# Scores from small square tiles, a rotated query layout, and a reordered start of the expert stage

## The chip, the cores and the metric

The kernel runs on one core of one Trainium2 chip. The metric is device time in microseconds (us). The core has TensorE (PE in the profile, with PEld for its weight loads), VectorE (DVE), ScalarE (ACT), GpSimd (POOL) and SyncE (SP), which issues most transfers. Each engine works through its own instructions in order, and waits where an operand or a buffer is not ready.

## The reference, cut to what matters

Three stages are computed one after the other: attention through a memory of 32 slots per head, a dense layer pair with ELU, and a layer with eight experts of which each token uses one.

```python
# attention: 8 batches x 8 heads, 576 rows, head size 64, 32 memory slots
a = softmax(phi, axis=rows)
k_m, v_m = a.T @ k, a.T @ v                  # 32 x 64 per head
attn = softmax(q @ k_m.T / 8)                # 576 x 32 per head
x = attn @ v_m                               # heads side by side: 4608 x 512
# dense: w_in 512 x 2048, w_out 2048 x 512 (given in double precision)
x = elu(x @ w_in) @ w_out
# experts: e = argmax of x @ w_gate, for each token
out = softmax(x @ w_gate)[e] * (relu(x @ w1[e]) @ w2[e])
```

## The kernel before, in words

**First part, attention and dense layer.** The work goes through 8 batches `b`; each has two halves `g` of 288 rows, and each half 16 steps `f` over slices of 128 of the 2048 inner columns. One step is `mm1` (L488, 6 matmuls of 288 columns, L496), `elu` and `split_g` on ACT, DVE and POOL, and `mm2` (L518, 12 matmuls, L528). `mm1` runs two steps ahead of `mm2`. A value is split in a rounded part and a rest, so that three fast products give a full-precision one. Beside the steps of batch b run, in small pieces, the attention of batch b+1 (`attn_items`, L725: pairs of a step and a function, for steps 0 to 31) and the rows of the finished half (`y_items`, L745: logits, ranks, and three `y_row` that turn 96 rows each and write them to a table in memory).

**Attention pieces.** Heads come in two groups u of four. `load_q` (L206) brings the queries of a group, 32 partitions per head, into half of a buffer `big`, of which there are two; `a4t` (L387) turns them in blocks of 32x32 on DVE into the other half (L390). `a3` (L355) sums keys and values per memory slot, `a3b` (L368) scales them into `kvm` on DVE (L372) and turns the keys block by block (L378) onto the diagonal of a 128x128 tile `bdk`, which is zero elsewhere. `a4` (L393) makes the scores: for each of two row halves g, two matmuls of the whole 128x128 array and 288 columns (L402), then a DVE transpose out of PSUM (L405). `a3c` (L380) turns the values on PE (L383) once both groups are scaled. `a6n` (L482) later multiplies the turned values by slices of w_in (`m_tiles`, L450, L458). In full precision each of these matmuls shows as two records in the trace.

**Order.** For batch 0, and the start of batch 1, the order is the written list `START`; `LATER` gives a few more pieces for steps of the rest of batch 1's work. From step 24 of the sequence on the kernel only lists the pieces; a scheduler of the framework orders each engine's instructions by what it believes to be ready, and earlier listed ones first. The order in the trace there is its own, not that of the list. Around the end of the last batch the order is written out again.

**PSUM.** The pool `ps_m` has two banks, shared by every piece beside `mm1` and `mm2`: the sums of `a3`, the scores, the turned values, the products of `a6n` (two banks at once), the logits, and `y_row`, whose bank ACT empties (L643).

**Second part, experts.** Tokens have been put in lists per expert (`itab`, written by `y_scatter`). Two blocks of 128 tokens ("early" slots) of the first expert are done before the full lists are known: their first products `early_mm1`, the turning of the result `early_hpose`, their second products `early_mm2`. The full lists are fetched by an indirect transfer into `its` (L1003), turned on PE by `columns` (L1053, L1057) into the index columns, and then `gather` (L1064) fetches the tokens of the next slots. `ctl_a`, `ctl_b`, `ctl_c` compute on DVE the control table that the engines read into registers for each slot. In the loop over slots, `slot(j)` runs `mm1` (L1098) and `mm2` of 128 tokens.

The calls at this seam, L1157 to L1175, and later L1209:

```python
split_lo(1, [0, 1, 3], first)      # POOL for even chunks, DVE for odd ones
split_lo(1, [2], first, V)
early_hpose(0)
...                                # early_mm1(1, 1, c)
columns()
gather(0)
split_lo(1, [4, 5, 7, 6], first)
gather(1); gather(2)
ctl_a(); ctl_b()
early_mm2(0); early_hpose(1); xpose(0); ctl_c()
early_mm2(1)                       # after the helpers of slot are defined
```

Of the kernel before, what the change touches and what calls it, by code (L numbers as in the profile page):

```python
# [24 lines left out]

START = """
q.0 phi.0 x.0 a1.0 kv.0 a1e.0 A0.0 a2.0.0 phi.1 A1.0.0 A1.0.1 a1.1 x.1 q.1 R.0.1 a4t.0 R.0.0 B.0 a2.0.1 a3.0 a1e.1
a2.1.0 kv.1 a3b.0 A0.1 a4t.1 A1.1.0 A1.1.1 R.1.0 x.2 a2.1.1 a4.0.0 a4.0.1 a5.0 a5e.0 a3.1 a3b.1 a5b.0 A0.2 R.1.1
a5m.0 a5c.0 a4.1.0 a5d.0 a4.1.1 x.3 a5.1 A1.2.0 A1.2.1 R.2.1 C.1 a5e.1 R.2.0 a3c A0.3 D.1.1 x.4 a5b.1 a5m.1 A1.3.0
A1.3.1 R.3.0 B.2 a5c.1 R.3.1 D.1.0 A0.4 A1.4.0 a5d.1 x.5 M.0 A1.4.1 x.6 R.4.1 R.4.0 C.3 B.4 D.3.0 Me.0 A0.5 A1.5.0  # L30
A1.5.1 R.5.1 D.3.1 mm1.0 R.5.0 mm1.1 A0.6 A1.6.0 A1.6.1 R.6.0 R.6.1 C.5 D.5.1 M.1 elu.0 elu.1 Me.1 g.0 M.2 Me.2
mm1.2 x.7 x.8 A0.7 x.9 A1.7.0 B.6 R.7.0 D.5.0 A1.7.1 g.1 elu.2 mm1.3 mm2.0 mm2.1 M.3 elu.3 Me.3 R.7.1 x.10 mm1.4
# [10 lines left out]
n.a5e.0 n.a3.1 n.a3b.1 n.a3c  # L43
"""
LATER = {
    23: "n.a5b.0 n.a5m.0 n.q2",
    24: "n.M.0 n.a5c.0",
    25: "n.pk2 n.a4.1 n.a5.1 n.a5e.1 n.a5b.1",
    27: "n.M.1",
    29: "n.a5d.0",  # L50
    30: "n.a5m.1 n.a5c.1 n.a5d.1",
# [6 lines left out]
def attn_moe_moe2_kernel(  # L58
# [13 lines left out]
    nc = tc.nc  # L72
# [89 lines left out]
    with ExitStack() as order:  # L162
        order.enter_context(tc.manual_schedule())
        setup()
        with ExitStack() as p1, ExitStack() as late_pool:
# [11 lines left out]
            wo = [  # L177
                wt0.rearrange("p y c a n -> p (y c) a n")[:, :, 1], pool.tile([P, NF, DM], F32R, name="wol"),
            ]
            bdk = pkp.tile([P, 2, P], F32, name="bdk")  # L180
            kvm = pkp.tile([P, 2, NQ, D], F32, name="kvm")

            win_t = {}
# [21 lines left out]

            def load_q(b, u):  # L206
                t = big()
                nc.sync.dma_start(out=t[:, 0], in_=q[b, 4 * u:4 * u + 4].rearrange("h (s j) d -> (h s) (j d)", j=NJ))
                q_t[b, u] = t

            conv_x, conv_h = {}, {}
# [156 lines left out]
            def a3b(b, u):  # L368
                ps, rs = st.pop(("kv", b, u)), st.pop(("rs", b, u))
                nc.vector.tensor_scalar(out=rs, in0=rs, scalar1=1e-9, scalar2=None, op0=ALU.add)  # L370
                nc.vector.reciprocal(out=rs, in_=rs)
                nc.vector.tensor_scalar(  # L372
                    out=kvm[:, :, u], in0=ps[:, 0:P].rearrange("p (y d) -> p y d", y=2), scalar1=rs, scalar2=None,
                    op0=ALU.mult,
                )
                for h in range(4):
                    r = slice(32 * h, 32 * h + 32)
                    nc.vector.transpose(out=bdk[r, :, r], in_=kvm[r, 0, u])  # L378

            def a3c(b):  # L380

# [8 lines left out]
                nc.vector.transpose(out=qT, in_=qt[:, 0].rearrange("p (j b d) -> p j b d", j=NJ, b=2))  # L390
                st["qT", b, u] = qT

            def a4(b, u, gs=range(2)):  # L393
                qT = st["qT", b, u]
                if gs[0] == 0:
                    st["sT", b, u] = pool.tile([P, NJ, M], F32, tag="aT", name="sT")
                sT = st["sT", b, u]
                n = NJ // 2
                for g in gs:
                    ps = ps_m.tile([P, 512], F32, tag="m", name="ps_s")  # L400
                    for db in range(2):
                        nc.tensor.matmul(  # L402
                            ps[:, 0:G], bdk[:, db, :], qT[:, n * g:n * g + n, db, :], start=(db == 0), stop=(db == 1)
                        )
                    nc.vector.transpose(out=sT[:, n * g:n * g + n], in_=ps[:, 0:G])  # L405

            def a5(b, u):
                sT = st["sT", b, u]
# [225 lines left out]

            def y_row(b, g, i):

                last = (b, g) == (B - 1, 1) and i > 0
                yr = (pool if last else late["p"]).tile([PK, DM], F32, tag=("yr", "a", "aT")[i * last], name="yr", bufs=1 if last else YR)
# [86 lines left out]
            def attn_items(b):  # L725

                t = [2, 3, 5, 5, 5, 4, 6, 7, 9, 9, 8, 10, 12, 11]
                t += [22, 23, 24, 26, 13, 22]
                it = [
                    (t[0], lambda: (a1(b, 0), a1e(b, 0))), (t[1], lambda: a2(b, 0)), (t[2], lambda: a3(b, 0)),  # L730
                    (t[2], lambda: load_pk(b, 1)), (t[3], lambda: a3b(b, 0)),
                    (t[4], lambda: (a1(b, 1), a1e(b, 1))), (t[5], lambda: a4t(b, 0)), (t[5], lambda: load_q(b, 1)),
                    (t[6], lambda: a2(b, 1)), (t[7], lambda: a4(b, 0)),
                    (t[8], lambda: a3(b, 1)), (t[9], lambda: (a3b(b, 1), a3c(b))),
                    (t[10], lambda: (a5(b, 0), a5e(b, 0))), (t[11], lambda: (a5b(b, 0), a5m(b, 0))),
                    (t[12], lambda: (a5c(b, 0), a5d(b, 0))), (t[13], lambda: a4t(b, 1)), (t[14], lambda: a4(b, 1)),
                    (t[15], lambda: (a5(b, 1), a5e(b, 1))), (t[16], lambda: (a5b(b, 1), a5m(b, 1))),
                    (t[17], lambda: (a5c(b, 1), a5d(b, 1))),
                ]
                if b + 1 < B:  # L740
                    it += [(t[18], lambda: load_pk(b + 1, 0)), (t[19], lambda: load_q(b + 1, 0))]
                it += [(NF + 4 * kk + 2, lambda kk=kk: a6n(b, kk)) for kk in range(NSL // 2)]
                return it

# [30 lines left out]
            def at(i, fn):  # L775
                bg.setdefault(i, []).append(fn)

            nc.gpsimd.memset(bdk, 0.0)
            todo = {}
            for u in range(2):  # L780
                for name, fn in (
                    ("phi", load_phi), ("kv", load_kv), ("q", load_q), ("a1", a1), ("a1e", a1e), ("a3", a3), ("a3b", a3b),
                    ("a4t", a4t), ("a5", a5), ("a5e", a5e), ("a5b", a5b), ("a5m", a5m), ("a5c", a5c),
                    ("a5d", a5d),
                ):
                    todo[f"{name}.{u}"] = lambda fn=fn, u=u: fn(0, u)
                for g in range(2):
                    todo[f"a2.{u}.{g}"] = lambda u=u, g=g: a2(0, u, [g])
                    todo[f"a4.{u}.{g}"] = lambda u=u, g=g: a4(0, u, [g])
# [29 lines left out]
            todo["n.q2"] = lambda: load_q(2, 0)  # L819
# [101 lines left out]
def phase2(nc, tc, a):  # L921
# [52 lines left out]
    with ExitStack() as p2:  # L974
# [148 lines left out]

        turn = [0]

        def mm2(get, half, at, ot=None):
            ps = ps_tile(ps_acc, f"acc{2 + turn[0]}")
            turn[0] = 1 - turn[0]
            i = 0
            for f in range(NF2):  # L1130
                for h, y in ((0, 0), (1, 0), (0, 1)):
                    nc.tensor.matmul(ps, get(h, f), half(wt[1][y][f]), start=(i == 0), stop=(i == 3 * NF2 - 1))  # L1132
                    i += 1
            if ot is None:
# [13 lines left out]

            hpose(src, lambda y, g: early_chunk(y, 2 * s + g))

        def early_mm2(s):
            def get(y, f):
                return early_chunk(y, 2 * s + f // 4)[:, P * (f % 4):P * (f % 4) + P]

            mm2(get, first, early_w[:, s:s + 1], early_f32(4 + s))

        split_hi(1, range(NCH), first)  # L1157
        for c in range(NC):
            early_mm1(1, 0, c)
        split_lo(1, [0, 1, 3], first)  # L1160
        split_lo(1, [2], first, V)
        early_hpose(0)
        for c in range(NC):
            early_mm1(1, 1, c)
        columns()
        gather(0)
        split_lo(1, [4, 5, 7, 6], first)
        gather(1)
        gather(2)
        ctl_a()  # L1170
        ctl_b()
        early_mm2(0)
        early_hpose(1)
        xpose(0)
        ctl_c()  # L1175
        def load_regs(j, cols, engines):
            return [
                nc.values_load(ctl[j:j + 1, c:c + 1], engines=engines, min_val=0, max_val=m) for c, m in cols  # L1178
# [27 lines left out]
            for i, (w, c) in enumerate(((w1, cv0), (w2, cv1))):  # L1206
                load_raw(nc, raw[i], w, ev, c)

        early_mm2(1)  # L1209
        cv, = load_regs(0, ((5, 1),), [SP])  # L1210
        ev = nc.values_load(ctl1[0:1, 0:1], engines=[SP], min_val=0, max_val=E - 1)
        for i, w in enumerate((w1, w2)):
# [62 lines left out]
```

## Time and profile before

| | before |
|---|---|
| median of 3 runs | 1434.15 us (1429.45 to 1438.15) |
| the profiled execution | 1433.82 us, of which 1431.8 us from the first to the last instruction |
| mean granted clock of TensorE | 0.969 of full speed |
| PE busy | 1311.6 us, 92% |
| DVE, ACT, POOL busy | 629.5, 636.0, 445.1 us |

The table gives busy time summed over all stages. The first 175 us are the start (written order, batch 0, conversion of the weights); from there to about 926 us run the steps; 926 to 953 us is the seam; from 953 us on the expert slots run.

### The profile page before, as it was taken

What the parts mean: (1) busy time and instruction counts of PE and PEld (TensorE: products, weight loads), DVE (VectorE), ACT (ScalarE), POOL (GpSimd) and SP (SyncE); (2) the same over time, 40 slices, a digit from 0 to 9 for tenths busy, and PEclk for the clock granted to TensorE, in tenths of its full rate; (3) what the DMA queues carried; (4) which work ended last, traced back from release to release, by engine and by line L of the source; (5) the groups of instructions that cost most, each with busy time, mean ns of one, the idle gap of its engine ahead of it and who ended that gap; (6) DMA issues with size and microseconds to landing.
All of it is one profiled execution on the core that took longest, in us unless ns stands there. A gap on an engine that the chain in (4) does not pass through costs nothing. (4 is left out here: it accounts for less than half of the span.)

```text
span 1431.8 us, 26774 instructions
## 1 busy us (share of the span) xinstructions
PE 1311.6 (92%) x9023; PEld 1139.3 (80%) x9023; DVE 629.5 (44%) x1337; ACT 636.0 (44%) x1377; POOL 445.1 (31%) x483
## 2 busy tenths in 40 slices
PE   3478799999999999899999989889999999999996
PEld 2267688898888898799899889768888888888885
DVE  4988564443443443434433323445222555252221
ACT  3567355564565555455555546414111444141110
POOL 2645343343343433333334334231111111111111
PEclk9699999999999999999999999989999999999998
DMA  9646655325324333323431500135111334211110
GB/s 243 186 153 185 204 100 139 87 82 100 87 82 100 100 79 91 109 77 106 108 73 38 164 20 25 23 133 200 39 38 46 121 142 152 101 40 38 44 46 30
DMA packets 55062, 140.68 MB, mean 98 GB/s; under 512 B 8809, under 2 KB 21226, under 8 KB 51312
## 3 DMA queue, kind: packets, MB, share of 16 engines
q1 hardware_dynamic: 46768, 118.15, 29.3%
q0 software_dynamic: 8128, 20.50, 4.4%
q8 instruction: 82, 1.34, 0.4%
q14 instruction: 84, 0.69, 0.2%
HBM read 253.79 MB, written 24.02 MB: 194 GB/s over the span
## 5 line engine op out<-in xcount | busy, mean ns | idle before, releaser
L513 POOL TENSOR_TENSOR gl<-e,gh 128x288 fp32r<-128x288 f32 x242 | 196.1, 813 | 395.8 <-ACT gh L512 316.2
L528 PE MATMUL ps_acc<-gl,wt 128*128 128x288 f32 x1024 | 308.1, 301 | 10.2 <-DVE gl L513 5.0
L528 PE MATMUL ps_acc<-gh,wt 128*128 128x288 f32 x1024 | 306.9, 300 | 3.3 <-ACT gh L512 3.3
L528 PE MATMUL ps_acc<-gh,wol 128*128 128x288 f32 x1024 | 305.6, 298 | 0.0
L496 PE MATMUL ps_h<-ath,wt 128*128 128x288 f32 x1024 | 262.7, 313 | 18.3 <-DVE e L505 18.3
L505 DVE SCALAR_TENSOR_TENSOR e<-e,ps_h 128x288 f32<-128x288 f32 x256 | 114.6, 449 | 257.2 <-ACT e L504 225.4
L496 PEld LDWEIGHTS ps_h<-ath,wt 128*128 128x128 f32 x1024 | 182.1, 193 | 56.2 <-issue 26.9
L528 PEld LDWEIGHTS ps_acc<-gl,wt 128*128 128x128 f32 x1024 | 196.6, 192 | 14.7 <-DVE gl L513 8.3
L528 PEld LDWEIGHTS ps_acc<-gh,wt 128*128 128x128 f32 x1024 | 197.1, 192 | 4.5 <-ACT gh L512 3.8
L528 PEld LDWEIGHTS ps_acc<-gh,wol 128*128 128x128 f32 x1024 | 196.7, 192 | 0.5 <-issue 0.5
L1098 PE MATMUL ps_h<-wt,xh 128*128 x592 | 195.0, 400 | 0.7 <-ACT hh L1114 0.7
L512 ACT CAST gh<-e 128x288 fp32r<-128x288 f32 x256 | 110.0, 431 | 154.7 <-DVE e L505 152.3
L1137 POOL DMA_INDIRECT out_dram<-ot,idw x37 | 37.8, 1021 | 384.0 <-DVE ot L1136 358.1
L496 PE MATMUL ps_h<-atl,wt 128*128 128x288 f32 x512 | 153.9, 301 | 0.0
L503 ACT ACTIVATE e<-ps_h 128x288 f32<-128x288 f32 x256 | 105.1, 410 | 92.4 <-PE ps_h L496 81.4
L1098 PEld LDWEIGHTS ps_h<-wt,xh 128*128 128x128 f32 x592 | 111.2, 188 | 26.1 <-ACT hh L1114 0.6
L1132 PE MATMUL ps_acc<-wt1h,hh 128*128 x296 | 120.9, 409 | 5.7 <-PEq L1178 5.7
L1132 PE MATMUL ps_acc<-wt1h,hl 128*128 x296 | 119.2, 403 | 0.0
L1114 ACT CAST hh<-ps_acc 128x512 fp32r<-128x512 f32 x74 | 39.8, 590 | 174.7 <-PE ps_acc L1112 174.6
L1132 PE MATMUL ps_acc<-wt1l,hh 128*128 x296 | 117.0, 395 | 0.0
L1098 PE MATMUL ps_h<-wt,xl 128*128 x296 | 116.9, 395 | 0.0
L504 ACT ACTIVATE e<-e 128x288 f32<-128x288 f32 x256 | 113.8, 444 | 7.0
(243 smaller groups left out, 1860.5 us busy)
## 6 DMA issues: line engine op xcount, KB each, us to landing
raw<-in_moe_w_dram SPq DMA_DIRECT2D x78, 2048.0 KB
win<-win_s SPq DMA_DIRECT2D x28, 1024.0 KB
big<-in_q_dram SPq DMA_DIRECT2D x16, 576.0 KB
kv<-in_k_dram SPq DMA_DIRECT2D x16, 576.0 KB
kv<-in_v_dram SPq DMA_DIRECT2D x16, 576.0 KB
table<-yr SPq DMA_DIRECT2D x144, 64.0 KB
big<-in_moe_w_out_dram SPq DMA_DIRECT2D x10, 512.0 KB
phi_t<-in_phi_dram SPq DMA_DIRECT2D x16, 288.0 KB
```

The lines of the kernel that those rows point to most:

```text
L496: nc.tensor.matmul(ps, x[:, u, fo:fo + P], y[:, u], start=(n == 0), stop=(n == 3 * NQ - 1))
L503: nc.scalar.activation(out=e, in_=ps, func=AF.Relu, scale=-1.0)
L504: nc.scalar.activation(out=e, in_=e, func=AF.Exp, scale=-1.0)
L505: nc.vector.scalar_tensor_tensor(out=e, in0=e, scalar=-1.0, in1=ps, op0=ALU.add, op1=ALU.max)
L512: nc.scalar.copy(out=gh, in_=e)
L513: eng.tensor_tensor(out=gl, in0=e, in1=gh.bitcast(F32), op=ALU.subtract)
L528: nc.tensor.matmul(acc[c], x[:, f, P * c:P * c + P], y, start=(first and n == 0), stop=(final and n == 2),)
L1098: nc.tensor.matmul(ps, x[:, c], half(wt[0][y][2 * c + hf]), start=(i == 0), stop=(i == 3 * NC - 1))
L1114: nc.scalar.copy(out=h, in_=ps)
L1132: nc.tensor.matmul(ps, get(h, f), half(wt[1][y][f]), start=(i == 0), stop=(i == 3 * NF2 - 1))
L1137: nc.gpsimd.indirect_dma_start(out=out, out_offset=IndirectOffsetOnAxis(ap=at, axis=0), in_=ot, in_offset=None, bounds_check=NT - 1, oob_i ...
```

## The change: what it does

Queries: `load_q` now brings the second row half of each group with its heads rotated by one place (head h in partitions 32((h+1) mod 4) on), in three transfers in place of one. In the list the load of the next batch's group 0 stands at step 8, one after the scores of the same group, and that of group 1 at step 23, one after the scores of group 1; before they stood at steps 22 and 4 (of the next batch).

Scores: `bdk` and its zeroing go. `a3b` writes `kT`: all four heads' keys in one transpose, and a second copy, rotated as the queries are, in four. `a4` uses 32x32 tiles: for each of two inner halves db, each g and each head a matmul of 288 columns, 16 in all, with g=0 in one PSUM bank and g=1 in the other; the two transposes out come after all of them.

Values: `a3c` is listed at step 10, no longer at 9 beside `a3b`.

Seam: all `split_lo` of the second weights go to DVE; `early_mm2(0)`, with `early_hpose(1)` inside it after its f=4, and `early_mm2(1)` are issued ahead of `xpose(0)`; `columns`, the gathers and `ctl_c` are issued inside `early_mm2(1)` after its f=3. The last two `y_row` use the same buffers as the others.

```diff
 def load_q(b, u):
     t = big()
-    nc.sync.dma_start(out=t[:, 0], in_=q[b, 4 * u:4 * u + 4].rearrange("h (s j) d -> (h s) (j d)", j=NJ))
+    src = q[b, 4 * u:4 * u + 4].rearrange("h (s j) d -> h s (j d)", j=NJ)
+    n = NJ * D // 2
+    for g, x, h, k in ((0, 0, 0, 4), (1, 1, 0, 3), (1, 0, 3, 1)):
+        nc.sync.dma_start(
+            out=t[32 * x:32 * (x + k), 0, n * g:n * g + n],
+            in_=src[h:h + k, :, n * g:n * g + n].rearrange("h s f -> (h s) f"),
+        )
 def a3b(b, u):
...
+    nc.vector.transpose(out=kT[:, 0], in_=kvm[:, 0, u])
     for h in range(4):
-        r = slice(32 * h, 32 * h + 32)
-        nc.vector.transpose(out=bdk[r, :, r], in_=kvm[r, 0, u])
+        x = 32 * ((h + 1) % 4)
+        nc.vector.transpose(out=kT[x:x + 32, 1], in_=kvm[32 * h:32 * h + 32, 0, u])
 def a4(b, u):
...
-    for g in gs:
-        ps = ps_m.tile([P, 512], F32, tag="m", name="ps_s")
-        for db in range(2):
-            nc.tensor.matmul(
-                ps[:, 0:G], bdk[:, db, :], qT[:, n * g:n * g + n, db, :], start=(db == 0), stop=(db == 1)
-            )
-        nc.vector.transpose(out=sT[:, n * g:n * g + n], in_=ps[:, 0:G])
+    ps = [ps_m.tile([P, 512], F32, tag="m", name="ps_s") for _ in range(2)]
+    for db in range(2):
+        for g in range(2):
+            for h in range(4):
+                r, m = slice(32 * ((h + g) % 4), 32 * ((h + g) % 4) + 32), slice(32 * h, 32 * h + 32)
+                nc.tensor.matmul(
+                    ps[g][m, 0:G], kT[r, g, db], qT[r, n * g:n * g + n, db, :],
+                    start=(db == 0), stop=(db == 1),
+                )
+    for g in range(2):
+        nc.vector.transpose(out=sT[:, n * g:n * g + n], in_=ps[g][:, 0:G])
 def attn_items(b):
...
-    (t[4], ...), (t[5], lambda: a4t(b, 0)), (t[5], lambda: load_q(b, 1)),
+    (t[4], ...), (t[5], lambda: a4t(b, 0)),
-    (t[8], lambda: a3(b, 1)), (t[9], lambda: (a3b(b, 1), a3c(b))),
+    (t[8], lambda: a3(b, 1)), (t[9], lambda: a3b(b, 1)), (t[9] + 1, lambda: a3c(b)),
-    it += [(t[18], lambda: load_pk(b + 1, 0)), (t[19], lambda: load_q(b + 1, 0))]
+    it += [..., (t[7] + 1, lambda: load_q(b + 1, 0)), (t[14] + 1, lambda: load_q(b + 1, 1))]
 # the seam
-split_lo(1, [0, 1, 3], first)
-split_lo(1, [2], first, V)
+split_lo(1, range(3), first, V)
 early_hpose(0)
+split_lo(1, range(3, NCH), first, V)
 for c in range(NC):
     early_mm1(1, 1, c)
-columns()
-gather(0)
-split_lo(1, [4, 5, 7, 6], first)
-gather(1)
-gather(2)
 ctl_a()
+early_mm2(0, {4: [lambda: early_hpose(1)]})
 ctl_b()
-early_mm2(0)
-early_hpose(1)
+early_mm2(1, {3: [columns, lambda: gather(0), lambda: gather(1), lambda: gather(2), ctl_c]})
 xpose(0)
-ctl_c()
...
-early_mm2(1)
```

## Rows read from the trace of the kernel before

**Rows 1.** The page: span, and busy time by engine.
```profile
span 1431.8 us, 26774 instructions
PE 1311.6 (92%) x9023; PEld 1139.3 (80%) x9023; DVE 629.5 (44%) x1337; ACT 636.0 (44%) x1377; POOL 445.1 (31%) x483
```
**Rows 2.** Busy time by stretch: stretch, length, PE, PEld, DVE, ACT, POOL, granted clock, DMA.
```profile
175.00:926.00 751.00, 719.43 (x5898) 656.27 (x5897) 313.84 (x819) 416.14 (x970) 285.74 (x339) 0.99 0.33 87
926.00:936.00 10.00, 0.45 (x2) 0.02 (x1) 0.91 (x2) 0.00 (x0) 2.73 (x2) 0.75 0.06 9
953.00:1416.00 463.00, 457.05 (x2194) 373.58 (x2192) 170.66 (x265) 124.93 (x228) 75.07 (x74) 1.00 0.25 88
```
**Rows 3.** Waits of PE, whole span: waiter, releaser, us in total, times, longest.
```profile
PE ps_v L383 <- DVE kvm L372: 6.4, 6, 1.3
...
PE ps_v L383 <- ACT yr L643: 0.7, 1, 0.7
...
PE ps_m L1057 <- DVE its L1055: 9.7, 1, 9.7
```
**Rows 4.** Timeline around 446 us: start, length, engine, line, operands, [idle before, releaser].
```profile
445.75 1.34 DVE L390 STREAM_TRANSPOSE big<-big 128x1152 f32<-128x1152 f32 x1
447.01 0.31 DVE L372 TENSOR_SCALAR kvm<-ps_kv,rs 128x128 f32<-128x128 f32 x1
447.47 0.30 PE L383 MATMUL ps_v<-ident,kvm 128*128 128x128 f32 x1 [1.19 <-DVE kvm L372]
```
**Rows 5.** Timeline around 482 us: scores of group 1, then the products of `a6n`.
```profile
481.41 2.11 PE L402 MATMUL ps_s<-big,bdk 128*128 128x288 f32 x8
483.45 1.73 PE L458 MATMUL ps_M<-win,vT 64*32 64x512 f32 x16
483.56 0.48 DVE L405 STREAM_TRANSPOSE sT<-ps_s 128x288 f32<-128x288 f32 x1 [0.49 <-PE ps_s L402]
```
**Rows 6.** Timeline of PE around 408 us: `a6n` with both banks free.
```profile
407.62 1.09 PE L458 MATMUL ps_M<-win,vT 64*32 64x512 f32 x16
408.64 0.40 PE L496 MATMUL ps_h<-ath,wt 128*128 128x288 f32 x1
```
**Rows 7.** Timeline around 538 us: scores of group 0 behind a `y_row`.
```profile
537.95 2.17 PE L402 MATMUL ps_s<-big,bdk 128*128 128x288 f32 x8
538.15 0.68 ACT L643 ACTIVATE yr<-ps_y,r_gate 96x512 f32<-96x512 f32 x1
```
**Rows 8.** Timeline around 486 us: a query load and its transpose.
```profile
483.55 0.35 SPq L208 DMA_DIRECT2D big<-in_q_dram  x1
489.94 1.38 DVE L390 STREAM_TRANSPOSE big<-big 128x1152 f32<-128x1152 f32 x1 [2.77 <-DMA big<-in_q_dram]
```
**Rows 9.** Waits of DVE, 200 to 860 us.
```profile
DVE big L390 <- DMA big<-in_q_dram: 17.6, 5, 5.3
```
**Rows 10.** Waits of PE, 280 to 700 us.
```profile
PE ps_h L496 <- DVE e L505: 12.3, 7, 3.9
```
**Rows 11.** Timeline of the seam, 922 to 952 us.
```profile
922.38 1.88 DVE L997 TENSOR_TENSOR wt1l<-raw,wt1h 128x512 fp32r<-128x512 f32 x3
923.44 3.01 PE L715 MATMUL ps_h<-wt 128*128 128x512 f32 x12
931.63 1.46 POOL L1003 DMA_INDIRECT its<-itab,rowi  x1 [9.40 <-issue]
935.75 0.22 DVE L1055 CAST its<-its 43x128 f32<-43x128 int32 x1 [8.57 <-DMA its<-itab,rowi]
936.93 1.38 POOL L1064 DMA_INDIRECT xg<-table,idx  x1 [2.54 <-DVE idw L1059]
942.67 0.16 DVE L963 SCALAR_TENSOR_TENSOR tmp<-en,ind 128x8 f32<-128x8 f32 x1
950.93 0.15 DVE L1051 CAST ctl<-e 128x1 int32<-128x1 f32 x1
952.32 0.39 PE L1098 MATMUL ps_h<-wt,xh 128*128 x1
```

More of the change, by code (lines that the diff above doesn't have):

```diff
@@ L27 @@
 q.0 phi.0 x.0 a1.0 kv.0 a1e.0 A0.0 a2.0.0 phi.1 A1.0.0 A1.0.1 a1.1 x.1 q.1 R.0.1 a4t.0 R.0.0 B.0 a2.0.1 a3.0 a1e.1
-a2.1.0 kv.1 a3b.0 A0.1 a4t.1 A1.1.0 A1.1.1 R.1.0 x.2 a2.1.1 a4.0.0 a4.0.1 a5.0 a5e.0 a3.1 a3b.1 a5b.0 A0.2 R.1.1
-a5m.0 a5c.0 a4.1.0 a5d.0 a4.1.1 x.3 a5.1 A1.2.0 A1.2.1 R.2.1 C.1 a5e.1 R.2.0 a3c A0.3 D.1.1 x.4 a5b.1 a5m.1 A1.3.0
+a2.1.0 kv.1 a3b.0 A0.1 a4t.1 A1.1.0 A1.1.1 R.1.0 x.2 a2.1.1 a4.0 a5.0 a5e.0 a3.1 a3b.1 a5b.0 A0.2 R.1.1
+a5m.0 a5c.0 a4.1 a5d.0 x.3 a5.1 A1.2.0 A1.2.1 R.2.1 C.1 a5e.1 R.2.0 a3c A0.3 D.1.1 x.4 a5b.1 a5m.1 A1.3.0
 A1.3.1 R.3.0 B.2 a5c.1 R.3.1 D.1.0 A0.4 A1.4.0 a5d.1 x.5 M.0 A1.4.1 x.6 R.4.1 R.4.0 C.3 B.4 D.3.0 Me.0 A0.5 A1.5.0
@@ L45 @@
 LATER = {
-    23: "n.a5b.0 n.a5m.0 n.q2",
+    23: "n.a5b.0 n.a5m.0 n.q2.0",
     24: "n.M.0 n.a5c.0",
     25: "n.pk2 n.a4.1 n.a5.1 n.a5e.1 n.a5b.1",
+    26: "n.q2.1",
     27: "n.M.1",
@@ L179, in attn_moe_moe2_kernel @@
             ]
-            bdk = pkp.tile([P, 2, P], F32, name="bdk")
+            kT = pkp.tile([P, 2, 2, M], F32, name="kT")
             kvm = pkp.tile([P, 2, NQ, D], F32, name="kvm")
@@ L391, in a4t, with a4 @@
                 st["qT", b, u] = qT
-            def a4(b, u, gs=range(2)):
+            def a4(b, u):
                 qT = st["qT", b, u]
-                if gs[0] == 0:
-                    st["sT", b, u] = pool.tile([P, NJ, M], F32, tag="aT", name="sT")
-                sT = st["sT", b, u]
+                sT = st["sT", b, u] = pool.tile([P, NJ, M], F32, tag="aT", name="sT")
                 n = NJ // 2
-                for g in gs:
-                    ps = ps_m.tile([P, 512], F32, tag="m", name="ps_s")
-                    for db in range(2):
-                        nc.tensor.matmul(
-                            ps[:, 0:G], bdk[:, db, :], qT[:, n * g:n * g + n, db, :], start=(db == 0), stop=(db == 1)
-                        )
-                    nc.vector.transpose(out=sT[:, n * g:n * g + n], in_=ps[:, 0:G])
+                ps = [ps_m.tile([P, 512], F32, tag="m", name="ps_s") for _ in range(2)]
[9 more added lines that the diff above has]
+                    nc.vector.transpose(out=sT[:, n * g:n * g + n], in_=ps[g][:, 0:G])
             def a5(b, u):
@@ L635, in y_row @@
             def y_row(b, g, i):
-                last = (b, g) == (B - 1, 1) and i > 0
-                yr = (pool if last else late["p"]).tile([PK, DM], F32, tag=("yr", "a", "aT")[i * last], name="yr", bufs=1 if last else YR)
+                yr = late["p"].tile([PK, DM], F32, tag="yr", name="yr", bufs=YR)
                 ysb = st["y", b, g]
@@ L727, in attn_items @@
                 t = [2, 3, 5, 5, 5, 4, 6, 7, 9, 9, 8, 10, 12, 11]
-                t += [22, 23, 24, 26, 13, 22]
+                t += [22, 23, 24, 26, 13]
                 it = [
@@ L731, in attn_items @@
                     (t[2], lambda: load_pk(b, 1)), (t[3], lambda: a3b(b, 0)),
-                    (t[4], lambda: (a1(b, 1), a1e(b, 1))), (t[5], lambda: a4t(b, 0)), (t[5], lambda: load_q(b, 1)),
+                    (t[4], lambda: (a1(b, 1), a1e(b, 1))), (t[5], lambda: a4t(b, 0)),
                     (t[6], lambda: a2(b, 1)), (t[7], lambda: a4(b, 0)),
-                    (t[8], lambda: a3(b, 1)), (t[9], lambda: (a3b(b, 1), a3c(b))),
+                    (t[8], lambda: a3(b, 1)), (t[9], lambda: a3b(b, 1)), (t[9] + 1, lambda: a3c(b)),
                     (t[10], lambda: (a5(b, 0), a5e(b, 0))), (t[11], lambda: (a5b(b, 0), a5m(b, 0))),
@@ L740, in attn_items @@
                 if b + 1 < B:
-                    it += [(t[18], lambda: load_pk(b + 1, 0)), (t[19], lambda: load_q(b + 1, 0))]
+                    it += [(t[18], lambda: load_pk(b + 1, 0)), (t[7] + 1, lambda: load_q(b + 1, 0)), (t[14] + 1, lambda: load_q(b + 1, 1))]
                 it += [(NF + 4 * kk + 2, lambda kk=kk: a6n(b, kk)) for kk in range(NSL // 2)]
@@ L776, in at @@
                 bg.setdefault(i, []).append(fn)
-            nc.gpsimd.memset(bdk, 0.0)
             todo = {}
@@ L782, in attn_moe_moe2_kernel @@
                     ("phi", load_phi), ("kv", load_kv), ("q", load_q), ("a1", a1), ("a1e", a1e), ("a3", a3), ("a3b", a3b),
-                    ("a4t", a4t), ("a5", a5), ("a5e", a5e), ("a5b", a5b), ("a5m", a5m), ("a5c", a5c),
-                    ("a5d", a5d),
+                    ("a4t", a4t), ("a4", a4), ("a5", a5), ("a5e", a5e), ("a5b", a5b), ("a5m", a5m),
+                    ("a5c", a5c), ("a5d", a5d),
                 ):
@@ L788, in attn_moe_moe2_kernel @@
                     todo[f"a2.{u}.{g}"] = lambda u=u, g=g: a2(0, u, [g])
-                    todo[f"a4.{u}.{g}"] = lambda u=u, g=g: a4(0, u, [g])
             todo["a3c"] = lambda: a3c(0)
@@ L818, in attn_moe_moe2_kernel @@
             todo["n.pk2"] = lambda: load_pk(2, 0)
-            todo["n.q2"] = lambda: load_q(2, 0)
+            for u in range(2):
+                todo[f"n.q2.{u}"] = lambda u=u: load_q(2, u)
             for kk in range(2):
@@ L1124, in phase2, with mm2 @@
         turn = [0]
-        def mm2(get, half, at, ot=None):
+        def mm2(get, half, at, ot=None, between={}):
             ps = ps_tile(ps_acc, f"acc{2 + turn[0]}")
@@ L1133, in mm2 @@
                     i += 1
+                for fn in between.get(f, ()):
+                    fn()
             if ot is None:
@@ L1149, in early_hpose, with early_mm2 @@
             hpose(src, lambda y, g: early_chunk(y, 2 * s + g))
-        def early_mm2(s):
+        def early_mm2(s, between):
             def get(y, f):
                 return early_chunk(y, 2 * s + f // 4)[:, P * (f % 4):P * (f % 4) + P]
-            mm2(get, first, early_w[:, s:s + 1], early_f32(4 + s))
+            mm2(get, first, early_w[:, s:s + 1], early_f32(4 + s), between)
         split_hi(1, range(NCH), first)
```

## The prediction, made before the changed kernel was run

> **What bounds the kernel now.** I read the page first [rows 1]: PE is busy for 1311.6 of 1431.8 us, the others for less than half. A sum over stages doesn't say where PE is missing, so the busy times by stretch come next [rows 2]. From 175 to 926 us PE works 719 of 751 us, in the expert slots 457 of 463, both at full clock: there TensorE is the bound, and the change can win only PE's own time or PE's waits. Between 926 and 936 us PE does 0.45 us of work, and the granted clock falls. Then PE's waits, by what ended them [rows 3, 9, 10], and the timeline around each. Three kinds lie where the change acts.
>
> 1. The turning of the values, L383, waits for DVE's `kvm`, 6.4 us in 6 waits, and 0.7 us once for ACT [rows 3]. The timeline shows why: DVE first turns queries (445.75 to 447.09), and only then makes `kvm` [rows 4]. PE stands meanwhile.
> 2. PE waits for DVE's `e` 12.3 us in 280 to 700 us [rows 10]. Five of these seven waits, 11.1 us together (the other two have 1.1), come right behind a query transpose for which DVE itself had waited, 17.6 us in five [rows 9]: the load was issued at 483.55, the transpose, ahead of `e` on DVE, started at 489.94 [rows 8].
> 3. At the seam PE waits 9.7 us in one piece for the token lists [rows 3, 11].
>
> **The values, a step later.** In the list L383 falls behind the rest of step 9 (the second part of `mm1`, and `mm2`). Before, it stood between the fourth and fifth matmul of that step's `mm1`; two more of these and 12 of `mm2`, at some 0.13 us from start to start, put it about 1.9 us later, against a wait of 1.19 [rows 4]. So the waits go: 6.4 of the six less 0.45 of one in the written part, which isn't moved, plus the 0.7: **-6.6 us**. What covers L383 is `mm2` of the same step; its result is wanted only at step 18. If the scheduler put it elsewhere the gain would be between 0 and 6.6; I take 6.6, as its instructions are then all ready.
>
> **The seam.** PE ends the first products at 926.45 [rows 11]. The lists can't come sooner: the fetch starts on POOL at 931.63 and DVE has it at 935.75. New is that PE goes on.
> - `early_mm2(0)`: 24 matmuls at 0.23 (12 of L715 took 2.88 to 3.01 [rows 11]) is 5.6 us, with `early_hpose(1)` in it 0.9: 926.5 to 933.0. What feeds it: eight `split_lo` on DVE at 0.63 (three in 1.88 [rows 11]), done by 928.7, with the transposes' rests between; the rest for chunk 3, f=3, is there at 926.2, PE wants it at 929.1. POOL's three `split_lo`, which stood behind the fetch, are gone.
> - `early_mm2(1)` up to f=3: 2.8 us, to 935.8. DVE has meanwhile the copy out (0.7 from 933.2) and `ctl_b`, 13 instructions at about 0.2 (it begins at 942.67 [rows 11]), to 936.7; the cast of the lists, behind it, comes at 936.7 in place of 935.75. PE waits 1.3 us, turns the lists at 937.1, and ends at 940.2.
> - The gather starts at 937.5 (before 936.93). The fetch of the lists took 4.1 us from start to use [rows 11]; with the same the tokens are there at 941.6, turned at 942.1, rounded by ACT at 942.8. The control table, 23 more instructions on DVE, is done at 941.0; before, 1.4 us lay between its last instruction and the slot's first matmul [rows 11], so it decides no more than the tokens.
> - The first slot starts at about 943.4 instead of 952.32: **-8.9 us**. Bounds: if tokens and table never hold PE, 940.5 (-11.8); if table or tokens take 1.1 us more, -7.8. The raw weights of the next expert wait for the second early slot's output and the table, and both move by as much.
>
> **The scores.** Four matmuls are 8 records of 0.24 us, 2.11 with the run-out [rows 5]. New are 16 matmuls, 32 records. The nearest row is `a6n`: 8 matmuls of 64x32 tiles and 512 columns, 16 records of 0.43 us, which would be 6.8 us in a row, take 1.09, and `mm1` starts 1.02 after them [rows 6]. Eight tiles do run side by side there. By that, the scores take 2 x 2 x 0.24 = 0.96, with 0.2 to 0.3 for the change of tile size. Bounds: 0.96, all side by side, and 32 x 0.24 = 7.7, none; I take 1.2, the row being near in shape. But it isn't 0.8 us won each:
> - Group 0 stands behind a `y_row`, which holds one of the two banks until ACT is through at 538.83 [rows 7]. The old order needs that bank only for its second half. The new one can do but the first eighth (0.5 us), waits to 538.9, and has 0.96 left: 539.9, where the old one ended at 537.95 + 1.93 = 539.9. Gain 0; 0.1 lost for the tiles.
> - Group 1 stands before `a6n`, which needs both banks emptied. Before, the second transpose ran at 483.56 to 484.04 [rows 5]. New: scores end at 482.6, run-out and two transposes of 0.48 after them, 483.8. Gain about 0.25 in each of six.
> Together **-1.5 us**. DVE gets one transpose of 0.24 more in each of 16 `a3b`, beside PE's work; in the start, where DVE is the busier engine, up to 0.5.
>
> **The queries.** The move itself does nothing: the load at 483.55 follows the last score matmul at 483.5 [rows 5, 8], and so do the other loads from batch 1 on. The scheduler already issued each load once its buffer was free, far ahead of its place in the list, and the transpose behind it. So the wait on DVE stays, for the other group's name. What differs: scores of group 1 end 0.9 us sooner against `a6n`, and the load with them; but three issues of 0.35 in place of one cost 0.7, and the bytes are the same. Per wait 0 to 0.9 us less; I take 0.4 in five: **-2 us**. From both sides: 11.1 us if the waits go; 7.5 more if the scheduler, which plans with smaller pieces, puts the transpose ahead of the two rests of `a6n` on DVE (then these 1.5 us also stand behind the wait, five times). At the very start two more issues ahead of the first `phi` load, and DVE's extra transposes: **+0.5 us**.
>
> The new `y_row` buffers and the dropped zeroing change nothing on PE's path.
>
> **Sum**, against the profiled execution's 1433.8 us (0.3 under the median): -6.6 - 8.9 - 1.5 - 2 + 0.5 = -18.5, **1415 us**.
>
> **Rivals.**
> - *The query waits go* (15%). For it: the scheduler plans three transfers otherwise than one, and the transpose needs to slip by only a few DVE instructions. Against: same bytes, same moment, same reach ahead. 9 us less than above: 1406.
> - *The scheduler's new order adds waits* (16%): the transpose gets ahead of `a6n`'s rests, or the values keep their wait. Up to 7.5 + 2 more: 1424.
> - *The seam hides less* (6%): the fetch of the lists waited 9.4 us on POOL for what the profile doesn't show [rows 11]; if that grows by half with the new order, 4.7 us come back: 1420.
> - *Slower: tiles of one bank take turns* (9%). In `a6n` each half of the rows has a bank of its own. In the new scores four row tiles write one bank, in different partitions, and no row here shows that. If they took turns, a round would last 4 x 0.24 x 2 and the scores 3.84 us in place of 1.93; with the change of tiles 2.1 us more in each of 13 in PE-bound steps, 27 us: 1442. It cancels the other gains from 3.2 us per score group on. The Trainium skill, "TensorEngine Tiling (Array Packing)", Gotcha 1: PSUM Pressure, has such a rule: different row tiles write to different PSUM banks, and can't access one bank at the same time. By that rule the time would be the 1442 of this rival; no row here shows it held or broken.
>
> **How the numbers follow.** The likeliest case (54%) is 1415, its own range 1409 to 1421. 8 in 10: the query and order rivals reach 1404 and 1427; I give 1403 to 1428 and leave out the slower rival. About 0.5% (7 us) is what can be told from no change: faster 0.85, within 0.08 (the order rival at its worst), slower 0.07.
>
> **What would show it.** Values: no wait on L383. Seam: no stretch of half clock, PE's list transpose inside the second early product, first slot 943 to 944 less what was won before. Scores: 32 records in 1.0 to 1.4 us for group 1 (near 4: the slower rival), group 0 with a gap. Queries: five DVE waits on the load still there. I'm wrong if PE's waits for `e` have gone, or if L402's successor takes over 2 us.

## The result, and the profile after

The changed kernel took 1411.63 us in the median of 4 runs (1410.08 to 1412.19), beside 1433.79 us of the kernel before: a ratio of 0.9844, 95% interval 0.9813 to 0.9875. Predicted were 1415 us. The profiled execution took 1412.19 us. The page's span and busy time, against [rows 1]:

```profile
span 1410.5 us, 27605 instructions
...
PE 1307.3 (93%) x9407; PEld 1124.6 (80%) x9407; DVE 626.2 (44%) x1356; ACT 634.7 (45%) x1377; POOL 437.3 (31%) x479
```

PE's busy time fell little (1311.6 to 1307.3): most of what went is time in which PE stood. The 21.3 us of the span by place, each from the starts of the same matmul in both timelines: the start, to the first scores of batch 2, is 2.2 longer (229.84 to 232.06); from there to the last scores of the loop 14.1 shorter (560.93 to 546.82); to the end of the loop 0.3 shorter; from the second group of early first products to the first matmul of the slots 9.3 shorter (28.9 us, [rows 11], to 19.6 by the seam's rows below); the slots 0.2 longer. Here are the busy times of that loop, from the first scores of batch 2 to the last scores, before and after (columns as in [rows 2]):

```profile
229.84:790.77 560.93, 537.90 (x4497) 490.34 (x4496) 233.65 (x586) 307.47 (x723) 213.94 (x252) 0.99 0.34 90
```

```profile
232.06:778.88 546.82, 532.13 (x4759) 478.30 (x4758) 232.16 (x597) 305.50 (x723) 213.48 (x252) 1.00 0.36 93
```

Of the 14.1 us, 8.3 are PE's idle time (23.0 to 14.7) and 5.8 its busy time. Most of the 5.8 is the clock: by an estimate like that of the last section, stretches at half clock cost some 6 us in the loop before, and 1.6 after (0.60 granted over 701 to 705 us).

PE's waits, 280 to 700 us (waiter, releaser, us in total, times, longest), against [rows 3, 10]:

```profile
PE ps_h L508 <- DVE e L517: 3.2, 5, 0.8
PE ps_y L653 <- DVE wt L480: 3.0, 5, 0.6
...
PE ps_s L412 <- ACT yr L654: 1.0, 1, 1.0
```

There is no wait for `kvm` in the loop any more, and the waits for `e` are 3.2 us where they were 12.3. But this stretch ends just ahead of the longest wait for `e`. Over the whole loop they are 6.4 us, against 12.3 before:

```profile
PE ps_h L508 <- DVE e L517: 6.4, 6, 3.1
```

That longest one stands behind another transfer on DVE, of `phi` and not of the queries:

```profile
697.54 0.78 DVE L335 STREAM_TRANSPOSE pT<-phi_t 128x576 f32<-128x576 f32 x1 [3.10 <-DMA phi_t<-in_phi_dram]
...
700.72 0.61 PE L508 MATMUL ps_h<-ath,wt 128*128 128x288 f32 x1 [3.11 <-DVE e L517]
```

New is `y_row`, which waits for the buffer that `a6n`'s evacuation on DVE frees, up to 0.6 each time. DVE itself still waits for the queries, as in [rows 9] (here 200 to 860 us), and then its timeline around 483 us, against [rows 8]:

```profile
DVE big L399 <- DMA big<-in_q_dram: 13.5, 6, 3.3
```

```profile
481.50 1.28 DVE L480 TENSOR_TENSOR wt<-ps_M,wt 128x512 fp32r<-128x512 f32 x2
482.69 0.44 DVE L517 SCALAR_TENSOR_TENSOR e<-e,ps_h 128x288 f32<-128x288 f32 x1
...
484.94 1.38 DVE L399 STREAM_TRANSPOSE big<-big 128x1152 f32<-128x1152 f32 x1 [1.72 <-DMA big<-in_q_dram]
...
486.39 0.40 DVE L517 SCALAR_TENSOR_TENSOR e<-e,ps_h 128x288 f32<-128x288 f32 x1
```

The transpose waits 1.72 us, but one `e` (482.69) now stands ahead of it. Before, the transpose came first and that `e` 1.3 us behind it. PE has a step in hand and doesn't stand.

The scores, PE's timeline: group 0 (at 431) against [rows 7], group 1 (at 476) against [rows 5].

```profile
431.27 1.15 PE L412 MATMUL ps_s<-big,kT 32*32 32x288 f32 x10
433.41 1.17 PE L412 MATMUL ps_s<-big,kT 32*32 32x288 f32 x22 [0.99 <-ACT yr L654]
...
475.96 1.20 PE L412 MATMUL ps_s<-big,kT 32*32 32x288 f32 x32
...
477.74 1.45 PE L470 MATMUL ps_M<-win,vT 64*32 64x512 f32 x16 [0.25 <-DVE sT L417]
```

32 records take 1.20 us. This group 0 stops after 10 of them for the bank that `y_row` holds. The other five in the loop run through and take 1.95 us to the next matmul; those that no bank held took 1.80 before. The seam, against [rows 11], and its granted clock (the column of 1.00), against the second line of [rows 2]:

```profile
910.14 1.88 DVE L1007 TENSOR_TENSOR wt1l<-raw,wt1h 128x512 fp32r<-128x512 f32 x3
911.21 3.01 PE L726 MATMUL ps_h<-wt 128*128 128x512 f32 x12
913.20 3.09 DVE L1007 TENSOR_TENSOR wt1l<-raw,wt1h 128x512 fp32r<-128x512 f32 x5
...
918.89 1.45 POOL L1013 DMA_INDIRECT its<-itab,rowi  x1 [8.89 <-DVE dp L1031]
924.70 0.25 PE L1067 MATMUL ps_m<-ident,its 43*128 43x43 f32 x1 [1.23 <-DVE its L1065]
929.37 0.66 PE L1085 MATMUL ps_m<-ident,xg 128*128 128x128 f32 x4 [1.42 <-DMA xg<-table,idx]
930.82 0.49 PE L1108 MATMUL ps_h<-wt,xh 128*128 x1 [0.80 <-ACT xh L1089]
```

```profile
914.00:924.00 10.00, 9.47 (x45) 7.44 (x44) 8.64 (x30) 1.08 (x2) 2.50 (x2) 1.00 0.11 35
924.00:932.00 8.00, 4.85 (x20) 3.32 (x21) 4.90 (x33) 0.59 (x1) 4.80 (x5) 1.00 0.40 119
```

PE goes from the first products (911.21) straight into the second ones, waits 1.23 us for the lists, and the half-clock stretch is gone.

### The profile page after: what moved, and what is told of

It reads as the page before. It is cut to its first block, busy times and chain, and to the rows that moved or that the text cites. A ratio compares the mean times of both kernels' runs of the same rounds, so it can differ in the third digit from the quotient of the medians.

```text
span 1410.5 us, 27605 instructions
## 1 busy us (share of the span) xinstructions
PE 1307.3 (93%) x9407; PEld 1124.6 (80%) x9407; DVE 626.2 (44%) x1356; ACT 634.7 (45%) x1377; POOL 437.3 (31%) x479
## 5 line engine op out<-in xcount | busy, mean ns | idle before, releaser
L508 PE MATMUL ps_h<-ath,wt 128*128 128x288 f32 x1024 | 262.0, 312 | 13.7 <-DVE e L517 13.5
```

The lines of the kernel that those rows point to most:

```text
L508: nc.tensor.matmul(ps, x[:, u, fo:fo + P], y[:, u], start=(n == 0), stop=(n == 3 * NQ - 1))
```

## The experiments

The runs came in three sets, on three chips, each with its own runs of the kernel before: 1437.88 us (values, seam's order, squares, order of the transpose), 1450.27 (seam with buffers, old row buffers, squares and values, old scores with the tie) and 1448.63 (the rest). Every ratio is to those of its own set. A single trace tells of waits and their causes, but not of a few us of gain: the loop of the kernel before took 560.9 us in its own trace and, with the same instructions in the same order, 568.5 and 574.0 in the two runs that changed the seam alone.

**The values alone.**

```diff
-    (t[8], lambda: a3(b, 1)), (t[9], lambda: (a3b(b, 1), a3c(b))),
+    (t[8], lambda: a3(b, 1)), (t[9], lambda: a3b(b, 1)), (t[9] + 1, lambda: a3c(b)),
```

> The kernel before, with a3c listed at step 10 in place of 9 and nothing else. Theory (the parts add up): the six PE waits for kvm at L383, 6.4 us, and the 0.7 us for ACT go, all but 0.45 us in the written part; the seven waits for e in 280 to 700 us stay at about 12 us, and the seam stays: -6.6 us, ratio 0.9954. Rival (the values' later place also breaks up the waits for e, so that it carries the loop's whole gain): waits for e under 5 us, -12 to -14 us, ratio 0.991. Rival (PE only waits for the same work a little later): ratio 0.999 to 1.000.

Measured: ratio 0.9928 (0.9908 to 0.9948), 10.3 us. PE's waits, 280 to 700 us:

```profile
PE ps_h L496 <- DVE e L505: 12.4, 7, 3.9
...
PE ps_v L383 <- DVE kvm L372: 0.3, 1, 0.3
```

The waits for `kvm` are gone and those for `e` untouched, so the first theory's mechanism holds and the rivals' do not. In time it is less clear: 0.9954 lies just outside the interval, the first rival's 0.991 inside. The loop of its trace took 554.69 us, 6.2 less than that of the kernel before, but 13.8 less than the old loop in a trace of its own set (568.5). Where the other 4 us of the gain are was not found.

**The seam's order alone** (new calls, `split_lo` on DVE; the last two `y_row` keep their own buffers).

> The kernel before, with the new order of the expert stage's start alone (rests of the second weights on DVE, both early second products ahead of the turned tokens, the table's pieces inside the second). Theory (the parts add up): first matmul of the slots 8.8 us after the change's trace, so 943.5 in place of 952.32, the loop untouched: -8.8 us, ratio 0.9939. Rival (the two y_row buffers, which are not changed here, are part of the seam's gain, since a row written later brings the lists later): -5 us, ratio 0.9965. No half-clock stretch between 926 and 936 by either.

Measured: 0.9995 (0.9980 to 1.0011): nothing. The theory and the rival both missed; the rival named the right buffers, but for another reason, and priced them at 3.8 us of the 8.8. The trace shows why, in the timeline of DVE and PE and in the busy times from 938 to 946 us:

```profile
940.51 1.90 DVE L997 TENSOR_TENSOR wt1l<-raw,wt1h 128x512 fp32r<-128x512 f32 x3 [6.00 <-DMA table<-yr]
...
943.06 1.11 PE L1112 MATMUL ps_acc<-ident,raw 128*128 128x128 f32 x4 [4.89 <-DVE raw L721]
```

```profile
938.00:946.00 8.00, 3.11 (x11) 2.55 (x10) 5.21 (x15) 1.17 (x2) 1.46 (x1) 0.73 0.02 3
```

The sixth rest waits 6.00 us for the transfer of a `y_row` into the table. It is to be written where that row still lies. Copying `early_mm1`'s result out stands behind it on DVE, PE waits 4.89 us for that, and the granted clock falls (0.73 over 938 to 946).

**The seam with the row buffers.** The edit added to the one above:

```diff
-    last = (b, g) == (B - 1, 1) and i > 0
-    yr = (pool if last else late["p"]).tile([PK, DM], F32, tag=("yr", "a", "aT")[i * last], name="yr", bufs=1 if last else YR)
+    yr = late["p"].tile([PK, DM], F32, tag="yr", name="yr", bufs=YR)
```

> The kernel before, with the new order of the expert stage's start and, unlike the run with that alone, the last two y_row in the same buffers as the others. Theory (the old buffers of those two rows are the room in which the rests of the weights are put, so that the rests waited 6.0 us on DVE for the rows' transfer): no wait of L997 on DVE for the transfer, no half clock at the seam, first matmul of the slots some 24.5 us after the last y_row as in the changed kernel (before 33.5, order alone 31.7): -8.8 us, ratio 0.9939. Rival (the transfer of the rows holds the seam whatever buffer they have, and the other parts of the change moved it out of the way): ratio 0.999 to 1.000, L997 waits again.

Measured: 0.9924 (0.9902 to 0.9947). No wait of DVE for the transfer is left, the clock is full to 956:

```profile
940.00:948.00 8.00, 8.00 (x40) 6.60 (x39) 6.74 (x25) 1.07 (x2) 2.22 (x2) 1.00 0.06 9
948.00:956.00 8.00, 4.55 (x21) 2.95 (x19) 5.14 (x37) 0.58 (x1) 4.20 (x5) 1.00 0.39 111
```

From the second group of early first products to the slots it takes 19.6 us here, 27.0 with the order alone, 28.9 before: the order alone brings 1.9, the buffers on top of it 7.4. The buffers with the old order were not run; in the trace before, no rest of a weight waits for a row's transfer.

**The changed kernel with the old row buffers** (the edit above taken back).

> The changed kernel, with the last two y_row back in their own buffers. Theory (as for the run before): L1007 on DVE waits 5 to 6 us for the transfer of the rows, PE stands in the first early second product and falls to half clock, +7 us on the changed kernel's 0.9844, ratio 0.989. Rival (the buffers don't matter once the loop ends sooner): ratio 0.984.

Measured: 0.9915 (0.9889 to 0.9941); the same way takes 27.5 us. The wait is back:

```profile
DVE wt1l L1008 <- DMA table<-yr: 6.9, 1, 6.9
```

So the theory holds from both sides, and in every trace: this way takes 28.9 to 31.2 us with the old order and the old buffers (five traces), 27.0 and 27.5 with the new order and the old buffers (two), 19.5 to 20.5 with both new (seven).

**The squares alone** (`load_q`, `a3b`, `a4` new; the loads' list places, the values and the seam old).

> The kernel before, with the square score tiles, the rotated layout and its three transfers alone; the loads keep their old places in the list, the values and the seam are as before. Theory (squares bring the loop's gain beside the values): PE's waits for e in 280 to 700 us fall from 12.3 to about 4, the six waits for kvm stay at about 6, the start is 2.2 us later: -21.3 + 6.6 + 8.8 = -5.9 us, ratio 0.9959. Rival (the loads' new places or the values' step did that): waits for e stay at 10 to 12, the scores' own 1.5 us against 2.2 us of the start: +0.7 us, ratio 1.0005. Group 1's 32 records in 1.2 us by both.

Measured: 1.0001 (0.9984 to 1.0017). PE's waits, 280 to 700 us:

```profile
PE ps_h L507 <- DVE e L516: 4.6, 5, 1.3
PE ps_v L391 <- DVE kvm L379: 4.0, 3, 1.6
PE ps_y L653 <- DVE wt L479: 2.8, 4, 0.9
```

The waits for `e` fall as the theory says, and yet nothing is won: `y_row` waits for `wt` (4.3 us in the whole loop), and the start is 4.0 us longer than before's, 2.8 longer than that of the seam's order in the same set. The theory's time falls; the rival's comes out, but not for its reason. That these two eat up the whole gain is not shown.

**Squares and values together.**

> The kernel before, with the square scores, their layout and loads, and the values a step later; the seam as before. Theory (the parts add): 0.9928 of the values alone times 1.0001 of the squares alone, ratio 0.993; PE waits for e in the loop 6 us, y_row waits for wt 6 us as with the squares alone, kvm none. Rival (the squares pay only with the values out of the way, since a wait for kvm right ahead of the scores moves everything behind it): the changed kernel less its seam, ratio 0.9844 + 0.0061 = 0.9905, y_row's wait for wt 3 us.

Measured: 0.9866 (0.9844 to 0.9888): more than the parts add up to, and more than the rival expected. In 280 to 700 us PE waits 5.5 us for `e`, 1.8 for `wt` and 0.8 for `kvm`. As the first two ran in another set, whose kernel before was 12 us faster, how much of this is interplay is not settled.

One thing stays open. This run and the changed kernel with the old row buffers are of one set, and up to the seam every engine has the same instructions in the same order. This one is slower at the seam (31.2 against 27.5), and yet faster by 6.9 us in the median; the loops of the two traces took 558.5 and 565.7. So what the buffers are worth is read from the seam's own times, not from 0.9915.

**The order of the transpose alone.** Old scores, old loads; one tie in the scheduler:

```diff
 def elu(b, g, f):
-    nc.vector.scalar_tensor_tensor(out=e, ...)
+    st["ei", b, g, f] = nc.vector.scalar_tensor_tensor(out=e, ...)
 def a4t(b, u):
-    nc.vector.transpose(out=qT, ...)
+    with tc.issue_after(st["ei", b - 2, 1, 8].ins) if u == 1 and b > 2 else ExitStack():
+        nc.vector.transpose(out=qT, ...)
```

> The kernel before, with one tie in the order and nothing else: the turning of group 1's queries, L390, may not be issued on DVE before the e of the first half's step 8 after it, so that one e and the sums stand ahead of it, as in the kernel after. Scores, loads and values are the old ones. Theory (the waits for e went because the scheduler put one more e ahead of the waiting transpose): DVE still waits for the queries five times, PE's waits for e in 280 to 700 us fall from 12.3 to 2 to 5, -7 to -8 us, ratio 0.995. Rival (they went because the scores are shorter and free the buffer sooner): PE waits for the next e instead, nothing gained, ratio 0.999 to 1.001.

Measured: 0.9926 (0.9909 to 0.9944), 10.6 us. PE's waits, 280 to 700 us, DVE's for the queries, and DVE's timeline:

```profile
PE ps_v L383 <- DVE kvm L372: 4.7, 4, 1.3
...
PE ps_h L497 <- DVE e L506: 0.8, 1, 0.8
```

```profile
DVE big L391 <- DMA big<-in_q_dram: 9.7, 6, 2.4
```

```profile
487.94 0.45 DVE L506 SCALAR_TENSOR_TENSOR e<-e,ps_h 128x288 f32<-128x288 f32 x1
...
489.91 1.38 DVE L391 STREAM_TRANSPOSE big<-big 128x1152 f32<-128x1152 f32 x1 [1.44 <-DMA big<-in_q_dram]
```

The transpose starts at 489.91, where it started at 489.94 before [rows 8]: the load is no sooner. But `e` goes out at 487.94, not 491.24, and all of PE's waits for `e` but one are gone. The theory holds, the rival falls; waits and time fall further than the theory said.

The loads' new list places need no run of their own: the trace of squares and values, with the old places, has the same instructions in the same order on all five engines as the changed kernel's, up to the seam.

**Old scores, with tie, values and the whole seam.**

> Without the squares: the kernel before, with the values a step later, the seam with its row buffers, and the tie that lets one e ahead of the waiting turn of the queries. Theory (the squares gave nothing but the order in which the scheduler then put the transpose, so old scores and the tie do the same or better): -10.3 (values) -10.6 (tie) -8.8 (seam) = -29.7 us of 1437.9 if all add, 1408, ratio 0.979; 0.982 if the gains of values and tie overlap by a half of the smaller. Rival (the shorter scores are worth something in the loop once the waits are gone): no faster than the changed kernel, ratio 0.985 or more.

Measured: 0.9839 (0.9816 to 0.9863). The gains don't all add. The value lies between the theory's 0.982 and the rival's 0.985, and the interval has both. Beside it, in the last set, the changed kernel itself, and this one again:

> The changed kernel again, beside the others on one chip, since the kernel before took 1433.8, 1437.9 and 1450.3 us in the three sets of runs so far and waits for transfers differ between them. If its parts add as on the last chip, 0.9866 (loop) times 0.9924 (seam), ratio 0.979; as in the first comparison, 0.984.

Measured: 0.9852 (0.9825 to 0.9879), as in the first comparison. The loop's and the seam's ratios of the set before would give 0.979, outside the interval: the parts, as measured one by one, don't multiply to the whole, and why is open.

> Old scores, values a step later, seam with its buffers, tie of the transpose behind one e; the same kernel as before, now beside the changed one. Theory (in the changed kernel the squares are worth no more than the order that came with them, and lose 2 to 4 us in the start): this one is faster than the changed kernel by 0.2 to 0.4%. Rival (the squares' shorter scores pay once the waits are gone, 1.5 us as predicted and more): slower than it by 0.1 to 0.4%.

Measured: 0.9838 (0.9811 to 0.9865). The two can't be told apart, so neither side is shown; what is shown is that the changed kernel's time is reached without its squares.

**No rotation.** The changed kernel with one transfer, one copy of the keys, and `r = m`: both row halves of a head through the same tile of the array.

```diff
-    r, m = slice(32 * ((h + g) % 4), 32 * ((h + g) % 4) + 32), slice(32 * h, 32 * h + 32)
+    r = m = slice(32 * h, 32 * h + 32)
```

> The changed kernel without the rotation: queries in one transfer, one copy of the keys, both row halves of a head through the same 32x32 tile of the array, so that only four tiles can work at a time. Theory (eight tiles work side by side in the changed kernel, the loads' pieces cost the start): group 1's 32 records take 2.1 to 2.3 us in place of 1.20, group 0's no longer than 2.3 (it waits for its bank anyway), +0.9 us in six; the start (first scores of batch 2) ends 2 to 4 us sooner than in the changed kernel; together -1 to +3 us against it. Rival (the tiles of a bank take turns at half, and rotation bought nothing): 1.2 to 1.3 us too, 3 us faster than the changed kernel. The transpose of the queries has one e ahead of it here too, so PE's waits for e are as in the changed kernel by both.

Measured: 0.9896 (0.9865 to 0.9926), 6.5 us over the changed kernel. Its group 1 scores:

```profile
481.28 2.14 PE L402 MATMUL ps_s<-big,kT 32*32 32x288 f32 x32
```

2.14 us against 1.20: four tiles at a time instead of eight, as the theory says. Its time (-1 to +3 us) did not come out. The sooner start is missing (228.9 us to the first scores of batch 2, 229.1 for the changed kernel in the same set), and group 0 isn't free: at the least it takes 2.43 us to the next matmul, 0.48 more than in the changed kernel. Group 1, to the end of `a6n` behind it, takes 0.60 more. By an estimate from these, six of each are 6.5 us. So within the squares eight tiles seem to be worth about that, though the two intervals touch. Beside the old scores they are not: those take 2.11 us too [rows 5], and with the tie they are as fast as the changed kernel. What the squares' form costs beside that is open.

**The tie behind two `e`** (step 9 in place of 8 in the tie, all else as with old scores, values and seam).

> The same, with the transpose tied behind two e in place of one. Theory (PE has one more step in hand, so that also a slow transfer of the queries doesn't reach it): the remaining waits for e right behind L390, up to 3.7 us in one, go, also the half-clock stretches behind them, another -4 to -8 us, ratio about 0.004 lower than with one. Rival (the kept buffer or the softmax behind it, whose parts now stand ahead, gives as much back): within 0.001 of the tie behind one.

Measured: 0.9754 (0.9727 to 0.9780), 1412.58 us where the changed kernel took 1426.27 in the same set: it beats both kernels. PE's waits for `e` in 280 to 700 us, behind one `e` (first line, four waits) and in the changed kernel of this set (second line); behind two there are none. The third line is DVE's wait for the queries in the changed kernel; with one `e` it is 21.2 us, with two 6.9.

```profile
PE ps_h L497 <- DVE e L506: 2.6, 4, 1.5
```

```profile
PE ps_h L508 <- DVE e L517: 6.9, 8, 1.4
```

```profile
DVE big L399 <- DMA big<-in_q_dram: 26.1, 10, 4.3
```

In this set DVE waits 26.1 us for the queries in the changed kernel, 13.5 in the first comparison. One `e` in hand leaves waits here; two leave none. The theory's waits go, but its size was too small (4 to 8 us expected, 12.1 measured against one `e`), and the half-clock stretches did not go: the granted clock of the whole trace is 0.970 with two, 0.971 with one.

Most of the rest lies in `a6n`, where the list of waits hardly shows it. With one `e`, five times in the loop, its products begin in one bank and then stop for the other, which `y_row` holds until ACT is through; 2.40 us pass to the next `mm1` in place of 1.02:

```profile
496.90 1.04 PE L459 MATMUL ps_M<-win,vT 64*32 64x512 f32 x2
497.55 0.68 ACT L643 ACTIVATE yr<-ps_y,r_gate 96x512 f32<-96x512 f32 x1
498.28 1.09 PE L459 MATMUL ps_M<-win,vT 64*32 64x512 f32 x14 [0.34 <-ACT yr L643]
```

With two `e` these five run through:

```profile
495.92 1.09 PE L459 MATMUL ps_M<-win,vT 64*32 64x512 f32 x16
```

Five times 1.38 is 6.9 us, beside 2.9 of waits for `e` in the whole loop; the loops of the two traces differ by 11.1 (556.8 and 545.6). So the second `e` pays also for a reason that the theory did not have: what moves with the transpose also meets `y_row`'s bank at another time.

## Why the prediction was right, and where it was not

The time came out (1415 against 1411.6), inside the range of the likeliest case. Its mechanism did so in part: the prediction gave as a sign of being wrong that PE's waits for `e` have gone, and most have: of 12.3 us in the loop 3.3 are left, beside the one behind `phi`. That the time fits all the same is partly luck. Step by step:

- **Values, -6.6: right in the waits.** None is left in the loop (6.6 us before: six waits for `kvm` less the written one, and one for ACT); the run with that edit alone left 0.3. Its time fell by 10.3 us, more than the term explains.
- **Seam, -8.9: right in size (9.3), wrong in one step.** "The new `y_row` buffers and the dropped zeroing change nothing on PE's path" failed: without these buffers the new order is worth 1.9 us, with them 9.3. My list of what feeds the second products had the engines and no memory: where the rests are written, and who still reads there. The wait for the lists came out as worked out: 1.23 us, predicted 1.3.
- **Scores: right in what they take, -1.5 not shown as a gain in time.** 1.20 us for 32 records. Group 0 was held by `y_row`'s bank in one of six, after 10 records (nearer a quarter than the "first eighth"); the others lose 0.15. Group 1 wins more than the 0.25 each: from its first matmul to the first `mm1` behind `a6n` it is 3.70 us before and 3.16 after, in all six, and one matmul of `mm1` has moved in between. But no run shows these as time beside the old scores. The slower rival, turns within a bank, is refuted: with eight tiles, four of them writing one bank in different partitions, 32 records take 1.20 us, with four tiles 2.14. The Trainium skill, "TensorEngine Tiling (Array Packing)", Gotcha 1: PSUM Pressure, says that different row tiles cannot access one bank at a time; for tiles that write different partitions this trace doesn't agree, and the measurement decides.
- **Queries, -2: the term that was mis-sized.** Half of it was right: the list places do nothing, the load is no sooner, and DVE waits for the queries six times, as it did five times before. "0.4 in five" failed. I carried DVE's wait over to PE. PE's wait is DVE's less the steps that PE has in hand, and the scheduler put one `e` ahead of the transpose. This is the first rival (15%), with its reason ("the transpose needs to slip by only a few DVE instructions"), although DVE's own waits stayed. The run with the tie alone won 10.6 us by it. In the changed kernel scores and queries together are -14.1 + 6.6 = -7.5 in the loop, where -3.5 was predicted and the first rival would have -12.6: other waits came in, for `wt` (3.0 us) and behind `phi` (3.1).
- **What the waits cost beside their length** was in no term: behind some waits the clock falls. By the estimate above this is some 4.5 of the loop's 14.1 us. See below.
- **Start, +0.5: mis-sized.** 2.2 us in these two traces. Single executions scatter: the five traces with the rotated layout reach batch 2's first scores at 229.1 to 233.9 us, the eight with the old scores at 227.5 to 232.6.

The errors had both signs: 4 us more in the loop, 1.7 less in the start, and a seam that was right only because an edit priced at nothing was there.

## What to carry to other kernels

A late operand on one engine costs the next engine only what it hasn't in hand: look at which instruction stands behind the waiting one, and put the work that others wait for ahead of it. Of a piece that is moved ahead, look also at the memory that it writes and at who still reads there. Before crediting a new form of the computation, hold the order of the old one: here the old scores with a tie behind one instruction reached the time of the new ones, and behind two were faster. And where PE's busy time differs between two orders, look inside it: a group of matmuls that stops halfway for a bank can count as busy.

## What was not expected of the hardware

Some waits of PE inside the loop are followed by a stretch at the lower of the clock's two levels (1.2 and 2.4 GHz), others are not. In the kernel before, those of 1.92, 3.86 and 3.38 us, which ended at 285.71, 595.72 and 699.54, are; those of 0.84 and 1.13 us, which ended at 389.45 and 491.71, are not. Its busy times behind the three (the granted clock is the third number from the right; none of these lines stood above):

```profile
286.00:290.00 4.00, 4.00 (x21) 3.99 (x21) 2.36 (x5) 1.79 (x6) 2.79 (x4) 0.60 0.02 7
596.00:600.00 4.00, 4.00 (x20) 3.76 (x20) 2.36 (x5) 1.80 (x6) 2.79 (x4) 0.57 0.11 42
700.00:704.00 4.00, 4.00 (x18) 3.98 (x18) 2.18 (x5) 1.79 (x6) 2.97 (x4) 0.50 0.02 6
704.00:708.00 4.00, 4.00 (x31) 3.67 (x37) 2.44 (x4) 3.14 (x8) 2.08 (x3) 0.79 0.20 46
```

At a mean of 0.57, 4 us carry 2.3 us of work at full clock: by this estimate 1.6 to 1.7 us are lost behind the first two waits, 2.0 + 0.8 behind the third. With the tie alone the stretches behind the same two transposes are at full clock; the longest wait there is 0.84 us:

```profile
594.00:598.00 4.00, 3.27 (x19) 2.58 (x20) 1.41 (x3) 1.96 (x6) 3.40 (x4) 1.00 0.19 74
694.00:698.00 4.00, 3.40 (x24) 2.92 (x23) 2.15 (x4) 1.29 (x4) 2.27 (x3) 1.00 0.50 197
```

So a wait that is cut from 3.86 us to 0.84 gives back more than its length. And the same program, the kernel before, took 1433.8 to 1450.3 us in four sets of runs; the changed one's DVE waited 13.5 us for the queries in one set and 26.1 in another. The last three sets ran on three chips; whether chip or time makes the difference is not shown. What an order with a step in hand is worth can differ as much.
